# Other landing times in the planner's model, and value loads behind the loads of q and k

## The chip, the cores and the metric

The kernel runs on one core of a Trainium2 chip. The core has five engines with an instruction stream each: PE (TensorE, matrix products), DVE (VectorE), ACT (ScalarE), POOL (GpSimd) and SP (SyncE, which here issues nearly all DMAs). Each takes its instructions in the order in which the program gives them, and waits at semaphores for the others. The metric is the device time of one execution in microseconds (us), the median of several runs.

## The reference

Thresholded attention, and after it a SwiGLU network on its output. q, k and v have 8 batches, 8 heads, 576 rows and 64 columns in float32; the network has 4608 tokens, a width of 512 and an inner width of 1536.

```python
scores = scale * np.matmul(q, k.transpose(0, 1, 3, 2))
thresh = np.max(scores, axis=-1, keepdims=True) - tau
scores = np.where(scores >= thresh, scores, -1000000000.0)
scores = scores - np.max(scores, axis=-1, keepdims=True)
attn = np.exp(scores)
attn = attn / (np.sum(attn, axis=-1, keepdims=True) + 1e-09)
x = np.matmul(attn, v)          # then heads side by side: (B * S, H * D)

xn = x / np.sqrt(np.mean(x * x, axis=-1, keepdims=True) + 1e-06) * rms_g
g, val = xn @ w_gate, xn @ w_val
out = (g * (1.0 / (1.0 + np.exp(-g))) * val) @ w_out
```

## The kernel before

**Steps.** The rows of attention are cut into 36 chunks of 128: four of each batch, and for each pair of batches one "virtual" chunk that holds the last 64 rows of both. A chunk times a pair of heads is a step, so there are 144 steps, numbered from 0. A step's score product runs on PE into PSUM (`emit_burst`, L680; `s_ps`). From step 32 on the scores of all steps are laid end to end and cut into bursts of 1024 columns. DVE scales a burst into `ssb` and keeps the row extreme (L713). POOL makes the threshold (`nth`, L754), ACT applies it and the exponential (L765, L769, L772), or for a third of the steps ACT makes the exponential (L784) and POOL the mask (L798, L803). The weights, `wsb` in float16, are turned by a DMA transposition on SP (L832; in the first 16 steps on PE, L817) into `wt`. Every second step PE multiplies two steps' `wt` by the values `va` (`emit_av`, L850 and L855), and DVE divides by the row sums (L872, L874). When a chunk has all its heads, ACT squares it (L896), POOL makes and applies the norm (L899 to L904), and a DMA transposition (L908) puts it into `xnT`. Groups of 2 or 4 chunks then go through the network on PE: gate (L962), value (L967) and output products (L1033; for the last group L1008 too), with ACT's tanh (L976), DVE's products (L979, L984) and evictions (L1046, L1048), and a store on SP (L1054, L1058).

**Inputs of a batch.** `emit_batch_inputs(b)` is called two batches ahead, and its loads are gated on score steps from the first step of batch b - 1 on. From batch 2 on (`BLOCKED = 2`) k comes in four loads of 288 KB and q in four more, in an order that DVE can turn by 32x32 blocks (`emit_block_loads`, L369). The turns (`emit_blocks`: `turn_k` L382, `turn_kt` L387, `turn_q` L392) are made once for each of four pairs of heads, and each waits for all four loads of its tensor. The values come in four loads of 256 KB (`load_block`, L589) and small ones for the last 64 rows (`load_tail`, L604), and POOL casts them to float16 (L565). Each of the four casts of a batch waits for all four loads, which in their turn wait for the previous batch's casts. The network's weights come in twelve loads of 512 KB at the start (L1099) and are cast by POOL (L1106).

**The order.** Every operation is an `Op` with an engine, a cost, a priority and its dependencies. `order_ops` (L55) walks through a model of the chip: at each moment it takes for every engine the operation that can start soonest, the lowest priority number first where several can, and gives it a start and an end. The order so found is the order of the instructions on each engine; the model's times decide nothing else. `RANK` adds a number to the priorities by engine and kind of operation (from priority 8 on). A priority counts score steps for the most part, so a number of some hundreds puts a kind ahead of, or behind, nearly all others. `gated(o, step)` adds to an operation the dependency on the score burst of the step int(step): its loads can't start before that. A DMA's end in the model is the time when a single shared transfer queue has done it, and a constant on top: `LAT_TR` for transpositions, `LAT_LD` for those marked `bulk`, 2000 ns for others. Bulk loads are held while the shared queue is over `BACKLOG` behind.

```python
if o.dma:
    dma_free = max(dma_free, t + 300.0) + o.dma
    o.end = max(dma_free, t + o.cost) + (LAT_TR if o.cost == COST["sp_tr"] else LAT_LD if o.bulk else 2000.0)
```

So the model says when a DMA's data are there, and whatever is placed behind on an engine's stream waits on the chip if they come later.

Of the kernel before, what the change touches and what calls it, by code (L numbers as in the profile page):

```python
# [17 lines left out]
    evac_qk=600.0, evac_qk_act=465.0, evac_half=252.0, evac_kt=330.0, evac_kt_act=252.0, prelu=667.0, exp2=1060.0, exp1=666.0, exp0=590.0,  # L18
    mask_d=680.0, mask_g=1810.0, take_g=1360.0, trw=510.0, evac_w=400.0, evac_wp=900.0, rz=210.0, xmul=341.0, sq=612.0, xn=773.0,
    pool_tiny=302.0, pool_mean=944.0, pool_dma=880.0, cast_v=620.0, cast_vt=475.0, cast_w=665.0,  # L20
    sp=420.0, sp_v=600.0, sp_w=600.0, sp_tr=1300.0, sp_qk=680.0, sp_tl=630.0, sp_qb=600.0, turn=600.0, turn_t=200.0, turn_q=665.0,
)
DMA_NS = dict(qkb=1900.0, qk=1250.0, tl=700.0, v=880.0, vt=350.0, wt=1700.0, xt=800.0, out=800.0, w=820.0, wo=2500.0)
SWITCH = 125.0

RANK = dict(
    ACT={"emit_ffn/ev": 120, "emit_ffn/store": 100, "emit_ffn/tanh": -230, "emit_k_tail/ev": -80, "emit_q_tail/ev": 170, "emit_qk/ev": 60,
        "emit_softmax/ex": -50, "emit_softmax/ex2": -210, "emit_softmax/prelu": -20, "emit_x/sq": -200},
    DVE={"emit_av/half": -4.4, "emit_blocks/turn_k": 2, "emit_blocks/turn_kt": 3, "emit_blocks/turn_q": 3, "emit_burst/ttr": -7.5, "emit_ffn/ev": 60,
        "emit_ffn/gate": -1.3, "emit_ffn/silu": -6.8, "emit_k_tail/ev": -90, "emit_qk/ev": -150, "emit_softmax/ev": 270},  # L30
    PE={"emit_av/fn": -190, "emit_burst/fn": -160, "emit_ffn/gmm": 5, "emit_ffn/omm": 12, "emit_ffn/vmm": -10, "emit_k_tail/tr": 10, "emit_q_tail/tr":
        -50, "emit_qk/tr": 80, "emit_softmax/tr": -220},
    POOL={"emit_softmax/mask": 50, "emit_softmax/nthr": -320, "emit_softmax/take": -150, "emit_x/mean": -50, "emit_x/norm": -80, "round_/<lambda>":
        -57, "main/<lambda>": 520, "main/cast": -360},
)


class Op:
    __slots__ = ("eng", "cost", "prio", "deps", "fn", "ring", "frees", "slot", "end", "start", "dma", "opens", "nring", "mode", "bulk", "release", "pick", "quad")

    def __init__(self, eng, cost, prio, deps, fn, ring=None, frees=None, dma=0.0, nring=1, mode=0, bulk=False):
        self.eng, self.cost, self.prio, self.fn = eng, cost, prio, fn
        self.deps = [d for d in deps if d is not None]
        self.ring, self.frees, self.dma = ring, frees, dma
        self.slot = self.end = self.start = None
        self.opens = ()
        self.nring = nring
        self.mode = mode
        self.bulk = bulk
        self.release = 0.0  # L50
        self.pick = None
        self.quad = False


def order_ops(ops, ring_sizes):  # L55


    import heapq

    for o in ops:  # L60
        if o.prio >= 8.0 and o.eng != "SP":
            path = o.fn.__qualname__.split(".")
            o.prio += RANK.get(o.eng, {}).get((path[-3] if path[-3].startswith(("emit", "load", "setup", "transposed", "round")) else "main") + "/" + path[-1], 0.0)

    ring_free = {r: [(0.0, i) for i in range(n)] for r, n in ring_sizes.items()}
    users = {}
    left = {}
    for i, o in enumerate(ops):
        left[i] = len(o.deps)
        for d in o.deps:  # L70
            users.setdefault(id(d), []).append(i)
    pending = {}
    for i, o in enumerate(ops):
        pending.setdefault(o.eng, [])
        if not left[i]:
            pending[o.eng].append(i)
    eng_free = {e: 700.0 for e in pending}
    dma_free = 0.0
    mode = 0
    out = []  # L80
    ready_at = {i: 0.0 for i in range(len(ops))}
    while len(out) < len(ops):
        best = None
        for e, lst in pending.items():
            if not lst:
                continue
            t0 = eng_free[e]
            cand = None
            opts = []
            for i in lst:  # L90
                o = ops[i]
                t = max(t0, ready_at[i])
                if o.ring is not None:
                    free = [f for f in ring_free[o.ring] if f[1] in (o.pick or SLOTS)]
                    if len(free) < o.nring:
                        continue
                    t = max(t, sorted(free)[o.nring - 1][0])
                other = e == "PE" and o.mode != mode
                t = max(t, o.release)
                if o.bulk:  # L100
                    t = max(t, dma_free - BACKLOG)
                t += BIAS if other else 0.0
                opts.append((t, o.prio, i))
            if opts:
                soon = min(opts)[0] + HOLD.get(e, 0.0)
                cand = min((x for x in opts if x[0] <= soon), key=lambda x: (x[1], x[0], x[2]))
            if cand is not None and (best is None or cand < best[0]):
                best = (cand, e)
        (t, _, i), e = best
        o = ops[i]  # L110
        cost = o.cost
        if e == "PE":
            if o.mode != mode:
                t -= BIAS
                cost += SWITCH
            mode = o.mode
        o.start = t
        if o.ring is not None:
            o.slot = []
            for _ in range(o.nring):  # L120
                got = min(f for f in ring_free[o.ring] if f[1] in (o.pick or SLOTS))
                ring_free[o.ring].remove(got)
                o.slot.append(got[1])
            if o.pick:
                o.slot.sort()
        eng_free[e] = t + cost
        if o.dma:
            dma_free = max(dma_free, t + 300.0) + o.dma
            o.end = max(dma_free, t + o.cost) + (LAT_TR if o.cost == COST["sp_tr"] else LAT_LD if o.bulk else 2000.0)
        else:  # L130
            o.end = t + cost
        if o.frees is not None:
            ring_free["R"].append((o.end + LAT[o.eng], o.frees[0].slot[o.frees[1]]))
        for slot in o.opens:
            ring_free["R"].append((o.end + LAT[o.eng], slot))
        pending[e].remove(i)
        out.append(o)
        for j in users.get(id(o), []):
            u = ops[j]
            wait = 60.0 if o.dma else SELF[o.eng] if u.eng == o.eng else LAT[o.eng]  # L140
            ready_at[j] = max(ready_at[j], o.end + wait)
            left[j] -= 1
            if not left[j]:
                pending[u.eng].append(j)
    return out
# [3 lines left out]
def kernel(  # L149
# [17 lines left out]
    NP = H // 2  # L167
# [80 lines left out]
    def gated(o, step):  # L248
        gates.append((o, step))
        return o  # L250
# [16 lines left out]
    for s, (ci, p) in enumerate(steps):  # L267
        kind, b, _ = chunks[ci]
# [90 lines left out]
    def emit_block_loads(b, prio):  # L359

        los = {}
        for j, src in ((1, k), (0, q)):
            before = turned[j] if turned else [x for t in tr_of for x in t[-NQK:]] + ([] if j else tail_load["use", 0])
            for h in range(2):
                for e in range(2):
                    def load(o, j=j, src=src, h=h, e=e):
                        rows = slice(64 * h + 32 * e, 64 * h + 32 * e + 32)
                        heads = src[b, NP * h:NP * h + NP, :, 32 * e:32 * e + 32]
                        nc.sync.dma_start(out=kx[rows] if j else qx[rows], in_=heads.rearrange("a (s r) d -> s r a d", r=RUN)  # L369
                                          if j else heads.rearrange("a (r s) d -> s a r d", r=RUN))  # L370

                    pr = prio + BLOCK_STEP * len([x for y in los.values() for x in y])
                    los.setdefault(j, []).append(gated(add("SP", COST["sp_qb"], pr, before, load, dma=DMA_NS["qkb"], bulk=True), pr))
        turned[:] = [[], []]
        return los

# [180 lines left out]
    def emit_v(b, prio):  # L557
# [10 lines left out]
        def free(p):  # L568
            return [o_v] + last_av.get((b - 2, p), [])

        for p in range(NP):
# [12 lines left out]
            if b >= BLOCKED and p == 0:  # L584
                lo = []
                for g in range(4):
# [2 lines left out]
                        nc.sync.dma_start(out=vst8[32 * g:32 * g + 32].rearrange("s h (c d) -> s h c d", d=D),  # L589
                                          in_=v[b].rearrange("h (s r) d -> s h r d", r=RUN)[:, :, at:at + 4])  # L590

                    lo.append(gated(add("SP", COST["sp_v"], pr + V_STEP * g, v_cast[-NP:], load_block, dma=DMA_NS['v'], bulk=True), pr + V_STEP * g))
            ca = add("POOL", COST["cast_v"], (pr + 1 if b else p - 1.0), lo + free(p), round_(
                t[:, p, 0:8, 0:D].rearrange("q (c h) d -> q h c d", h=2),
                nat.rearrange("q h (c d) -> q h c d", d=D)))
            v_cast.append(ca)
# [495 lines left out]
    for c in range(DFF // 512):  # L1092
        for d in range(0, 4, 2):
            for w_dram, w_sb in ((moe_w_gate, wg), (moe_w_val, wv)):
# [5 lines left out]
                        "(e p) n -> p e n", p=128))  # L1100

                lo = gated(add("SP", COST["sp_w"], pr, w_use[slot], load, dma=2 * DMA_NS['w'], bulk=True), pr)
                w_use[slot] = []
                for e in range(2):
                    def cast(o, d=d, w_sb=w_sb, c=c, slot=slot, e=e):
# [71 lines left out]
PART_PRIO = 2.0  # L1177
SIZES = (2, 2, 4, 4, 4, 4, 4, 4, 4, 4)
LAG = 8.0
LAT_TR = 3000.0  # L1180
LAT_LD = 2000.0
REL = (0.0, 0.0)
REL_N = (0, 0)
# [17 lines left out]
NSTAGE = 3  # L1201
NQK = 3
BLOCKED = 2
BLOCK_STEP = 1.5
V_STEP = 1.5
W_FROM = 2.0
W_STEP = 0.4
N_XPE = 0
# [41 lines left out]
```

## Time and profile before

| | us |
|---|---|
| median of 13 runs | 562.21 |
| lowest and highest of them | 558.0 and 565.13 |
| the profiled execution | 558.0 |
| its span | 556.1 |

The span is the time from the first to the last instruction of the program in the trace. PE is busy for 528.5 us of it, DVE 463.9, ACT 424.3, POOL 256.0. A transfer's time "to landing" runs from its issue on SP to the last byte. "Idle before" is the time for which an engine stood still just ahead of an instruction, put down to what came last. Matmul ends are modelled, so PE's holes are read from the starts of the matmuls.

### The profile page before, as it was taken

The page shows a single profiled execution, that of the slowest core. Times are in us where ns is not written, and L with a number is a line of the kernel's source. Part 1 is how long each engine was busy: PE and PEld are TensorE (multiplying, and loading weights), DVE is VectorE, ACT ScalarE, POOL GpSimd, SP SyncE. Part 2 cuts the span into 40 slices and gives each one's busy share as a digit, 9 for nine tenths or more (in the row PEclk, how much of TensorE's full clock was granted, in tenths as well). Part 3 has the DMA queues.
Part 4 walks back from the last instruction along what each step waited for, and adds up shares of the span by engine and source line. Part 5 has one row for each costly group of instructions (what it writes and reads, how often), then busy time and mean ns, then how long its engine had stood idle before and what let it go on. Part 6 is the DMA issues. An engine that isn't in the chain of part 4 may idle for free.

```text
span 556.1 us, 14272 instructions
## 1 busy us (share of the span) xinstructions
PE 528.5 (95%) x5336; PEld 277.9 (50%) x5336; DVE 463.9 (83%) x1342; ACT 424.3 (76%) x648; POOL 256.0 (46%) x418
## 2 busy tenths in 40 slices
PE   8989999896998999899999999999999999999997
PEld 4765656553554554454444444544454545445443
DVE  4997989674999798888998899879987997995481
ACT  5998988577897787958895798877976897994230
POOL 2377823473446544355446455364435535361100
PEclk9999999998999999999999999999999999999999
DMA  9999999989999998999999799999999667575202
GB/s 212 241 296 275 161 143 173 171 158 155 164 171 145 158 159 151 183 176 176 172 177 181 161 150 156 179 214 152 148 187 191 139 101 135 98 112 118 86 1 77
DMA packets 325318, 89.03 MB, mean 160 GB/s; under 512 B 307840, under 2 KB 317568, under 8 KB 325248
## 3 DMA queue, kind: packets, MB, share of 16 engines
q1 hardware_dynamic: 322320, 85.76, 91.2%
q0 software_dynamic: 1600, 1.57, 1.9%
q8 instruction: 42, 0.69, 0.6%
q10 hardware_dynamic: 1328, 0.79, 0.5%
q14 instruction: 28, 0.23, 0.1%
HBM read 37.75 MB, written 9.44 MB: 85 GB/s over the span
## 4 chain that ended last, share of the span: by engine, by line
PE 48%; DVE 15%; DMA 10%; ACT 5%; issue 3%; SPq 2%; POOL 2%; DVEq 0%; POOLq 0%; ACTq 0%
PE s_ps L680 14%; PE ring L1033 9%; PE ring L967 8%; PE ring L962 8%; DVE ssb L713 8%; DMA wt<-wsb 4%; DMA qkx<-in_q_dram 4%; PE ring L855 3%; PE s_ps L1008 2%; ACT ssb L765 2%; DVE sl L979 2%; DVE qkt L392 1%; PE s_ps L1033 1%; PE ring L850 1%; ACT wsb L772 1%
## 5 line engine op out<-in xcount | busy, mean ns | idle before, releaser
L765 ACT ACTIVATE ssb<-ssb,nth 128x576 f32<-128x576 f32 x246 | 180.2, 766 | 28.5 <-POOL nth L754 28.4
L680 PE MATMUL s_ps<-qkt 64*64 64x288 f32 (+9 forms) x2240 | 177.2, 415 | 11.2 <-DVE mxp L713 7.2
L713 DVE CUSTOM_DVE_ANT_0 ssb<-s_ps,zrow 128x576 f32<-128x576 f32 (+8 forms) x288 | 170.6, 635 | 11.3 <-PE s_ps L680 6.1
L772 ACT ACTIVATE wsb<-ssb 128x1152 f16<-128x1152 f32 x102 | 118.0, 1157 | 16.1 <-DMA wt<-wsb 15.1
L680 PEld LDWEIGHTS s_ps<-qkt 64*64 64x64 f32 (+1 forms) x2240 | 84.7, 135 | 77.6 <-issue 26.7
L967 PE MATMUL ring<-xnT,wv 128*128 128x512 f16 (+1 forms) x460 | 108.1, 357 | 1.7 <-DVE sl L979 1.0
L754 POOL TENSOR_SCALAR nth<-mx 128x2 f32<-128x2 f32 x144 | 31.6, 219 | 168.4 <-DVE mx L713 163.4
L962 PE MATMUL ring<-xnT,wg 128*128 128x512 f16 (+1 forms) x460 | 108.0, 357 | 0.9 <-DVE sl L979 0.7
L798 POOL TENSOR_SCALAR wsb<-ssb,nth 128x576 f16<-128x576 f32 x42 | 72.5, 1726 | 23.0 <-DMA wt<-wsb 18.0
L976 ACT ACTIVATE th<-ring 128x512 f32<-128x512 f32 (+1 forms) x115 | 61.8, 539 | 24.6 <-PE ring L962 24.5
L979 DVE SCALAR_TENSOR_TENSOR sl<-th,ring 128x512 f32<-128x512 f32 (+1 forms) x115 | 71.1, 621 | 8.0 <-ACT th L976 8.0
L713 DVE CUSTOM_DVE_ANT_0 ssb<-s_ps,zrow,mxp 128x128 f32<-128x128 f32 (+7 forms) x112 | 52.9, 510 | 21.1 <-PE s_ps L680 21.0
L962 PEld LDWEIGHTS <-wg 128*128 128x128 f16 x480 | 44.2, 98 | 52.1 <-issue 10.4
L967 PEld LDWEIGHTS <-wv 128*128 128x128 f16 x480 | 43.7, 98 | 53.1 <-issue 14.6
L803 POOL TENSOR_TENSOR wsb<-wsb,esb 128x576 f16<-128x576 f16 x42 | 53.8, 1280 | 3.4
L855 PE MATMUL ring<-va,wt 128*128 128x65 f16 (+1 forms) x1280 | 51.5, 193 | 0.0
L855 PEld LDWEIGHTS <-wt 128*128 128x128 f16 (+1 forms) x1280 | 46.3, 100 | 7.7 <-issue 3.8
L1033 PE MATMUL ring<-wo,hf 128*128 128x512 f16 x204 | 47.2, 379 | 2.1 <-DVE xsb L874 1.7
L784 ACT ACTIVATE esb<-ssb,nth 128x576 f16<-128x576 f32 x42 | 32.3, 770 | 15.9 <-POOL nth L754 15.8
L850 PE MATMUL ring<-va,wt 128*128 128x130 f16 (+1 forms) x160 | 32.2, 224 | 6.8 <-DVE sl L979 3.4
L984 DVE TENSOR_TENSOR hf<-ring,sl 128x512 f16<-128x512 f32 (+1 forms) x59 | 36.6, 627 | 1.9
L984 DVE TENSOR_TENSOR stg<-ring,sl 128x512 f16<-128x512 f32 (+1 forms) x56 | 34.4, 625 | 2.3 <-PE ring L967 0.5
(73 smaller groups left out, 499.3 us busy)
## 6 DMA issues: line engine op xcount, KB each, us to landing
vst<-in_v_dram SPq DMA_DIRECT2D x32, 256.0 KB, 4.5
out_dram<-osb SPq DMA_DIRECT2D x29, 256.0 KB, 2.5
qkx<-in_k_dram SPq DMA_DIRECT2D x24, 288.0 KB, 4.7
qkx<-in_q_dram SPq DMA_DIRECT2D x24, 288.0 KB, 5.2
stg<-in_moe_w_gate_dram SPq DMA_DIRECT2D x6, 512.0 KB, 6.3
stg<-in_moe_w_val_dram SPq DMA_DIRECT2D x6, 512.0 KB, 6.2
wt<-wsb SPq DMA_TRANSPOSE x128, 4.0
qkx<-in_k_dram SPq DMA_DIRECT2D x7, 256.0 KB, 4.9
```

The costliest lines, as they stand in the source:

```text
L680: nc.tensor.matmul(s_ps[h][rows, at:at + hi - lo], lhs(hs), k_of(bb, p, h)[hs, lo:hi], start=True, stop=True)
L713: nc.vector.tensor_tensor_reduce(out=ssb_of(s)[:, h, lo:hi], in0=s_ps[h][:, at:at + hi - lo], in1=zrow[:, lo:hi], scale=-1.0 / 8.0, scalar ...
L765: nc.scalar.activation(out=sb_[:, h], in_=sb_[:, h], func=PRELU, scale=-1.0, bias=nth[m][:, h:h + 1], **PRELU_KW)
L772: nc.scalar.activation(out=wsb[s % NW], in_=sb_, func=AF.Exp)
L798: nc.gpsimd.tensor_scalar(out=wsb[s % NW][:, h], in0=sb_[:, h], scalar1=nth[m][:, h:h + 1], scalar2=None, op0=ALU.is_le)
L855: nc.tensor.matmul(ring[o.slot[0]][rs, at:at + D + 1], w[:, 5 * h + j, rs], va[vi][:, p, 2 * j + h], start=False, stop=(h == 1 and j == 3))
L962: nc.tensor.matmul(ring[o.slot[0]][:, 0:n], wg[d][:, fs], xnT[slot][:, d, 0:n], start=(d == 0), stop=(d == 3))
L967: nc.tensor.matmul(ring[o.slot[0]][:, 0:n], wv[d][:, fs], xnT[slot][:, d, 0:n], start=(d == 0), stop=(d == 3))
L976: nc.scalar.activation(out=th[i][:, 0:n], in_=ring[g.slot[0]][:, 0:n], func=AF.Tanh, scale=0.5)
L979: nc.vector.scalar_tensor_tensor(out=sl[i][:, 0:n], in0=th[i][:, 0:n], scalar=1.0, in1=ring[g.slot[0]][:, 0:n], op0=ALU.add, op1=ALU.mult)
L984: nc.vector.tensor_tensor(out=hf[hi][:, 0:n], in0=ring[vv.slot[0]][:, 0:n], in1=sl[i][:, 0:n], op=ALU.mult)
L1033: nc.tensor.matmul(ring[(first or o).slot[0]], hf[hs[fc][0]][:, 128 * j:128 * (j + 1)], wo[:, fc], start=(fc == 0), stop=(fc == NFC - 1))
```

## The change

The planner's model gets a landing time for each kind of load: `Op` has a field `lat`, with new constants for the block loads of q and k (`LAT_QB`, 4500 ns), of values (`LAT_V`, 4000) and of the network's weights (`LAT_W`, 3000), all 2000 before. `LAT_TR` goes from 3000 to 2000. The value loads of a batch are gated `V_FROM` = 6 steps later and then one step apart instead of 1.5; the block loads of q and k stand 1.4 steps apart instead of 1.5. The casts of the values get a priority `V_CAST` = 9 later instead of 1, from batch 2 on. Two costs of the model change slightly, and all numbers of `RANK`. No instruction computes anything else than before.

```diff
-    ... turn_t=200.0, turn_q=665.0,
+    ... turn_t=210.0, turn_q=680.0,
 RANK = dict(
-    ACT={"emit_ffn/ev": 120, "emit_ffn/store": 100, "emit_ffn/tanh": -230, "emit_k_tail/ev": -80, "emit_q_tail/ev": 170, "emit_qk/ev": 60,
-        "emit_softmax/ex": -50, "emit_softmax/ex2": -210, "emit_softmax/prelu": -20, "emit_x/sq": -200},
-    DVE={"emit_av/half": -4.4, "emit_blocks/turn_k": 2, "emit_blocks/turn_kt": 3, "emit_blocks/turn_q": 3, "emit_burst/ttr": -7.5, "emit_ffn/ev": 60,
-        "emit_ffn/gate": -1.3, "emit_ffn/silu": -6.8, "emit_k_tail/ev": -90, "emit_qk/ev": -150, "emit_softmax/ev": 270},
-    PE={"emit_av/fn": -190, "emit_burst/fn": -160, "emit_ffn/gmm": 5, "emit_ffn/omm": 12, "emit_ffn/vmm": -10, "emit_k_tail/tr": 10, "emit_q_tail/tr":
-        -50, "emit_qk/tr": 80, "emit_softmax/tr": -220},
-    POOL={"emit_softmax/mask": 50, "emit_softmax/nthr": -320, "emit_softmax/take": -150, "emit_x/mean": -50, "emit_x/norm": -80, "round_/<lambda>":
-        -57, "main/<lambda>": 520, "main/cast": -360},
+    ACT={"emit_ffn/ev": 260, "emit_ffn/store": 60, "emit_ffn/tanh": -350, "emit_k_tail/ev": -140, "emit_q_tail/ev": -100, "emit_qk/ev": 280,
+        "emit_softmax/ex": 18, "emit_softmax/ex2": -350, "emit_softmax/prelu": 18, "emit_x/sq": -320},
+    DVE={"emit_av/half": -10.4, "emit_blocks/turn_k": 30, "emit_blocks/turn_kt": 20, "emit_blocks/turn_q": 50, "emit_burst/ttr": -14.1, "emit_ffn/ev":
+        140, "emit_ffn/gate": -80, "emit_ffn/silu": -13.4, "emit_k_tail/ev": -130, "emit_qk/ev": -100, "emit_softmax/ev": 410},
+    PE={"emit_av/fn": -260, "emit_burst/fn": -160, "emit_ffn/gmm": 18.5, "emit_ffn/omm": 22, "emit_k_tail/tr": 250, "emit_q_tail/tr": -200,
+        "emit_qk/tr": 170, "emit_softmax/tr": -190},
+    POOL={"emit_softmax/mask": 110, "emit_softmax/nthr": -180, "emit_softmax/take": -170, "emit_x/mean": -60, "emit_x/norm": -41, "round_/<lambda>":
+        -47.8, "main/<lambda>": 670, "main/cast": -260},
 )
...
+        self.lat = LAT_TR if cost == COST["sp_tr"] else LAT_LD if bulk else 2000.0
...
-            o.end = max(dma_free, t + o.cost) + (LAT_TR if o.cost == COST["sp_tr"] else LAT_LD if o.bulk else 2000.0)
+            o.end = max(dma_free, t + o.cost) + o.lat
...
                     los.setdefault(j, []).append(gated(add("SP", COST["sp_qb"], pr, before, load, dma=DMA_NS["qkb"], bulk=True), pr))
+                    los[j][-1].lat = LAT_QB
...
-                    lo.append(gated(add("SP", COST["sp_v"], pr + V_STEP * g, v_cast[-NP:], load_block, dma=DMA_NS['v'], bulk=True), pr + V_STEP * g))
-            ca = add("POOL", COST["cast_v"], (pr + 1 if b else p - 1.0), lo + free(p), round_(
+                    pl = pr + V_FROM + V_STEP * g
+                    lo.append(gated(add("SP", COST["sp_v"], pl, v_cast[-NP:], load_block, dma=DMA_NS['v'], bulk=True), pl))
+                    lo[-1].lat = LAT_V
+            ca = add("POOL", COST["cast_v"], (pr + V_CAST if b >= BLOCKED else pr + 1 if b else p - 1.0), lo + free(p), round_(
...
+                lo.lat = LAT_W
...
-LAT_TR = 3000.0
+LAT_TR = 2000.0
...
-BLOCK_STEP = 1.5
-V_STEP = 1.5
+BLOCK_STEP = 1.4
+V_STEP = 1.0
+V_FROM = 6.0
+V_CAST = 9.0
+LAT_QB = 4500.0
+LAT_V = 4000.0
+LAT_W = 3000.0
```

More of the change, by code (lines that the diff above doesn't have):

```diff
@@ L20 @@
     pool_tiny=302.0, pool_mean=944.0, pool_dma=880.0, cast_v=620.0, cast_vt=475.0, cast_w=665.0,
-    sp=420.0, sp_v=600.0, sp_w=600.0, sp_tr=1300.0, sp_qk=680.0, sp_tl=630.0, sp_qb=600.0, turn=600.0, turn_t=200.0, turn_q=665.0,
+    sp=420.0, sp_v=600.0, sp_w=600.0, sp_tr=1300.0, sp_qk=680.0, sp_tl=630.0, sp_qb=600.0, turn=600.0, turn_t=210.0, turn_q=680.0,
 )
@@ L26 @@
 RANK = dict(
-    ACT={"emit_ffn/ev": 120, "emit_ffn/store": 100, "emit_ffn/tanh": -230, "emit_k_tail/ev": -80, "emit_q_tail/ev": 170, "emit_qk/ev": 60,
-        "emit_softmax/ex": -50, "emit_softmax/ex2": -210, "emit_softmax/prelu": -20, "emit_x/sq": -200},
-    DVE={"emit_av/half": -4.4, "emit_blocks/turn_k": 2, "emit_blocks/turn_kt": 3, "emit_blocks/turn_q": 3, "emit_burst/ttr": -7.5, "emit_ffn/ev": 60,
-        "emit_ffn/gate": -1.3, "emit_ffn/silu": -6.8, "emit_k_tail/ev": -90, "emit_qk/ev": -150, "emit_softmax/ev": 270},
-    PE={"emit_av/fn": -190, "emit_burst/fn": -160, "emit_ffn/gmm": 5, "emit_ffn/omm": 12, "emit_ffn/vmm": -10, "emit_k_tail/tr": 10, "emit_q_tail/tr":
-        -50, "emit_qk/tr": 80, "emit_softmax/tr": -220},
-    POOL={"emit_softmax/mask": 50, "emit_softmax/nthr": -320, "emit_softmax/take": -150, "emit_x/mean": -50, "emit_x/norm": -80, "round_/<lambda>":
-        -57, "main/<lambda>": 520, "main/cast": -360},
+    ACT={"emit_ffn/ev": 260, "emit_ffn/store": 60, "emit_ffn/tanh": -350, "emit_k_tail/ev": -140, "emit_q_tail/ev": -100, "emit_qk/ev": 280,
[6 more added lines that the diff above has]
+        -47.8, "main/<lambda>": 670, "main/cast": -260},
 )
 class Op:
-    __slots__ = ("eng", "cost", "prio", "deps", "fn", "ring", "frees", "slot", "end", "start", "dma", "opens", "nring", "mode", "bulk", "release", "pick", "quad")
+    __slots__ = ("eng", "cost", "prio", "deps", "fn", "ring", "frees", "slot", "end", "start", "dma", "opens", "nring", "mode", "bulk", "release", "pick", "quad", "lat")
     def __init__(self, eng, cost, prio, deps, fn, ring=None, frees=None, dma=0.0, nring=1, mode=0, bulk=False):
```

## The prediction

> **What bounds the kernel now.** I read the page first (engines, slices, DMA issues), then the waits by engine, then the timeline wherever PE stood still.
>
> ```profile
> span 556.1 us, 14272 instructions
> ...
> PE 528.5 (95%) x5336; PEld 277.9 (50%) x5336; DVE 463.9 (83%) x1342; ACT 424.3 (76%) x648; POOL 256.0 (46%) x418
> ...
> DMA  9999999989999998999999799999999667575202
> ...
> vst<-in_v_dram SPq DMA_DIRECT2D x32, 256.0 KB, 4.5
> ...
> qkx<-in_q_dram SPq DMA_DIRECT2D x24, 288.0 KB, 5.2
> ...
> wt<-wsb SPq DMA_TRANSPOSE x128, 4.0
> ```
>
> PE is nearly full, and the DMA engines are as full until the last loads. So no engine has spare work to lose: a gain has to come out of PE's holes. Adding up every place where a matmul starts over 0.25 us later than the columns of the one before it account for gives 26.8 us, of which 21.5 us lie between 84 and 440 us, where the loads run. Three kinds stand out.
>
> First, loads that land on the dot. On DVE, on POOL, and SP's queue before them (timeline rows: start, length, instruction, idle before it):
>
> ```profile
> 105.86 0.78 DVE L392 STREAM_TRANSPOSE qkt<-qkx 128x576 f32<-128x576 f32 x1 [3.73 <-DMA qkx<-in_q_dram]
> ```
> ```profile
> 301.07 2.76 DVE L392 STREAM_TRANSPOSE qkt<-qkx 128x576 f32<-128x576 f32 x4 [2.59 <-issue]
> ```
> ```profile
> 298.99 1.80 POOL L565 TENSOR_SCALAR va<-vst 128x512 f16<-128x512 f32 x3 [1.91 <-DMA vst<-in_v_dram]
> ```
> ```profile
> 294.92 0.58 SPq L589 DMA_DIRECT2D vst<-in_v_dram  x1
> 295.55 0.46 SPq L369 DMA_DIRECT2D qkx<-in_q_dram  x1
> 296.18 4.84 SPq L832 DMA_TRANSPOSE wt<-wsb  x2
> ```
>
> Batch 5's last value load and last q load are issued side by side at 294.9 and 295.6 us. They land at 298.75 and 300.99; the cast starts at 298.99 and the turn of q at 301.07. So it is in nearly every batch: the last q lands at 105.83, 173.15, 245.12, 300.99, 372.38, 427.45 us and the first turn starts at 105.86, 173.34, 245.20, 301.07, 372.84, 427.53. The "issue" that ends the 2.59 us is that landing. DVE's idle time before these turns is 3.73, 0.35, 1.94, 2.59, 0 and 0.07 us.
>
> Second, a place with no filler (stretches: length; busy us by engine; granted clock; DMA):
>
> ```profile
> 126.00:129.50 3.50, 0.91 (x10) 0.46 (x6) 2.56 (x11) 1.97 (x3) 1.64 (x4) 1.00 0.92 190
> 129.50:132.30 2.80, 2.78 (x50) 2.19 (x50) 0.75 (x3) 2.77 (x5) 2.63 (x2) 1.00 1.07 181
> 132.30:135.00 2.70, 0.16 (x6) 0.03 (x2) 2.67 (x13) 2.13 (x4) 0.82 (x3) 1.00 0.81 136
> 135.00:139.00 4.00, 3.94 (x18) 1.41 (x19) 0.36 (x4) 2.14 (x3) 0.00 (x0) 0.57 1.16 153
> ```
> ```profile
> 129.52 2.23 PE L680 MATMUL s_ps<-qkt 64*64 64x384 f32 x32 [2.62 <-DVE mxp L713]
> ...
> 135.06 3.68 PE L680 MATMUL s_ps<-qkt 64*64 64x512 f32 x16 [2.60 <-DVE mxp L713]
> ```
>
> Around steps 39 and 40 score bursts follow each other with nothing, or only attention times values, between. PE waits twice for DVE to empty the scores' PSUM, and then the granted clock falls to 0.57 for 4 us; a burst that takes 1.89 us elsewhere takes 3.68.
>
> Third, PE waiting for a transposed weight tile, still small:
>
> ```profile
> L850 PE MATMUL ring<-va,wt x160: 217/220/245, 19.3 to 513.2; 128*128 128x130 f16 x128, 128*64 128x130 f16 x32
> ...
>   DMA wt<-wsb: 5.2, 9
> ```
>
> **What the Trainium skill says.** [...]"DMA: Bandwidth & Descriptors", Queues, rings and completion order: SP has one ring on each DMA engine, consumed in order, so a transposition of SP stands behind SP's loads; here they take 3.2 us at the least, 4.0 in the median, 8.7 at most. "TensorE: Matmul & The Clock Gate", What's actually happening: the array's clock is halved after an idle window of about 3.4 us; the 0.57 after holes of 2.6 us twice agrees.
>
> **The change part by part.** No instruction's arithmetic changes; only the order and the gates do. Compared step by step, 439 of 593 PE steps, 711 of 864 on DVE and 194 of 321 on SP move, on PE mostly by up to three places.
>
> *q earlier (counted 6.7 us from issue at the least instead of 4.2; measured 5.2).* The value loads leave the gaps between the q loads. Counting by score step, the last q load of batches 2 to 7 stood behind transposition 24, 43, 64, 80, 101, 116 and now behind 24, 41, 61, 77, 97, 113. The first turn of q stood behind eviction 29, 49, 69, 85, 106, 120 and now behind 29, 47, 67, 83, 103, 119. The distance was 5, 6, 5, 5, 5, 4 steps and is 5, 6, 6, 6, 6, 6. A step is 3.6 us (some 520 us over 144), so one step more covers the waits of batches 4 and 5 (1.94, 2.59). What PE lost to them is 1.5 us at 250 us and 0.43 + 0.48 us at 306 to 307.5: -2.4 us. Batch 2 keeps its distance, but its last q has no value load straight before it; I count part of its holes (1.6 and 0.7 at 105 to 108) with those after the turns of batches 3, 6 and 7 (1.8, 1.2, 1.2, 0.8): -1.5 us out of 7, bounds 0 and -5.
>
> *The place without filler.* Before step 40's burst there now stand a gate and a value product, 8 matmuls of 216 ns, 1.7 us that came later. Step 39 stays bare. The hole shrinks by 1.7 us unless their xnT is late (it landed at 133.4, so 1 us of it would stay). If the clock then stays up, 1.8 us more. I take -3.0; bounds -1.7 and -4.6.
>
> *Early filling.* Between steps 15 and 33 one more FFN product (4 x 109 ns) and six more output products (6 x 216 ns) are done, less a transposition that moves away: -1.2 us if they fall into the early holes, 0 if DVE, which evicts them, was the limit there.
>
> *Attention times values sooner.* The transpositions' constant falls from 3.0 to 2.0 us; the planner thus counts 4.0 us from issue at the least and no longer 5.0. The measured median is 4.0, so half of them are now later than counted. In the new order these matmuls stand on average 1.4 us of PE work nearer to their burst, since bursts move back. I took for the 64 groups from step 17 on the start of the first matmul on the pair's second tile less that tile's landing: a tenth have under 0.26 us, a quarter under 1.2, half under 2.2. Pulling all of them 0.5 us forward costs the sum of the shortfalls, 3.3 us; 1.0 us costs 9.4. Cover that hides it: none, PE is full. I take 0.5, because transpositions land after 3.6 to 3.9 us where no loads run against 4.2 to 4.8 where they do, and loads no longer pair up: +3.3, bounds 0 and +9.4.
>
> *Values later (counted at least 5.2 us instead of 3.2; measured 4.5).* From last load to first cast there were 6, 4, 4, 4, 3, 4 steps and are 4, 3, 3, 4, 6, 4 (batch 3's other casts 5). POOL already idled 0.5 to 1.9 us at these casts. Queued behind them are the thresholds (L754), and ACT's prelu waits for those. A threshold late by 3.25 us at 221 us (tail values) left PE holes of 1.2, 0.5 and 0.7 us. Attention times values itself has many steps to spare. +1.0 us; bounds 0 and +3.
>
> *The rest.* PE changes mode 162 times instead of 157, about 0.1 us each (the median gap into a burst): +0.5. Weight loads keep their order and stay hidden behind the first bursts; uncovered they would cost at most POOL's 4.3 us of waits for them.
>
> Sum: -2.4 -1.5 -3.0 -1.2 +3.3 +1.0 +0.5 = -3.3 us. The profiled execution took 558.0 us (span 556.1), the lowest of 13; the median is 562.2. The difference carries over: **558.9 us**.
>
> **Rivals.**
> *Transpositions become the bound (slower).* Place: the wait of L850 for wt. All 64 groups lose the full 1.0 us that the constant gives away: +9.4, with +3 at the casts, +0.5, and -8.1 of gains: +4.8, 567 us. For it: a median landing equal to the count leaves no margin, and the order really moves. Against: loads bunch less. With the other terms as taken it decides from a pull of about 0.8 us on.
> *Nothing comes of it (same).* The q turns are no longer late, but DVE then waits for PE instead (it already does for 27 us before L713), and the casts take the place of the turns: 562 us.
> *More than I count.* All batch holes go with the q waits (-7 rather than -3.9), the clock stays up (-4.6), the transpositions land as counted (+1): about -11, 551 us. Against: holes at 222 and 370 us come from tail values and from output stores, which the change doesn't aim at.
>
> **How the numbers follow.** Forecast, a gain of 2 to 8 us: 0.41. More: 0.15. Same, within 0.3% or 1.7 us, about what a measurement of this kernel can tell from no change: 0.17. Slower: 0.27. So faster 0.56, same 0.17, slower 0.27. The range runs from 549.5 (a little past the larger gain) to 568 (past the slower case), leaving out about 1 in 10 at each end; the forecast's own range is 554 to 560.5.
>
> **What would show it.** Right: no DVE idle time over 1 us before L392 in batches 4 to 7; one hole, not two, near steps 39 and 40, and no stretch at clock 0.57; more waits of L850 for wt than 5.2 us, but under 9. Wrong: L850's waits over 12 us; POOL idle over 10 us before L565, with ACT's waits for the thresholds grown from 44 us; or new bare bursts, which the order does not show.

## The result, and the profile after

The changed kernel takes 557.03 us (median of 11 runs, 553.69 to 560.02) against 562.27 for the kernel before (48 runs). The ratio is 0.9898, with a 95% interval from 0.9877 to 0.9919: 5.2 to 5.7 us faster, depending on whether medians or the ratio are taken. A second comparison, further down, gave 0.9873 (0.9837 to 0.9910). The profiled execution took 556.28 us, its span 554.5. Since the profiled execution before was the fastest of its runs, the two profiles lie only 1.7 us apart, and they are compared here mainly by kinds of waits. A second profile of the changed kernel (after_again, 553.4 us) is used where one profile misleads.

The page of the changed kernel:

```profile
span 554.5 us, 14260 instructions
...
PE 523.2 (94%) x5336; PEld 274.9 (50%) x5336; DVE 467.7 (84%) x1342; ACT 427.0 (77%) x648; POOL 255.9 (46%) x418
...
DMA  8999999989999999999999699999999676754102
...
vst<-in_v_dram SPq DMA_DIRECT2D x32, 256.0 KB, 4.6
...
qkx<-in_q_dram SPq DMA_DIRECT2D x24, 288.0 KB, 5.4
...
wt<-wsb SPq DMA_TRANSPOSE x128, 3.9
```

Amounts of work and transfers are the same, and the landing times hardly differ: 4.6 for 4.5, 5.4 for 5.2, 3.9 for 4.0 us. The loads did not become quicker by being spread; they are asked for at other moments. (Lines shift: L392 is now L394, L565 L567, L713 L717, L850 and L855 are L854 and L859, L872 L876, L962 L966.)

The turns of q of batch 5 and its first casts, on DVE's and POOL's timelines (start, length, instruction, idle before it):

```profile
288.09 2.09 DVE L394 STREAM_TRANSPOSE qkt<-qkx 128x576 f32<-128x576 f32 x3
```
```profile
301.44 1.80 POOL L567 TENSOR_SCALAR va<-vst 128x512 f16<-128x512 f32 x3 [0.52 <-DMA out_dram<-osb]
```

No turn of any batch has idle time before it any more; the last q of batch 5 lands at 286.05, 2 us before its turn (in batches 2 to 7 0.4 to 5.1 us before). The idle time that stood there, 8.6 us over the six batches, is gone. The casts, later as they are, wait less than before: POOL's idle time before L567 is 9.0 us against 14.8.

What has come in its place is seen in the query for PE's value matmuls:

```profile
L854 PE MATMUL ring<-va,wt x158: 217/221/290, 18.8 to 507.6; 128*128 128x130 f16 x126, 128*64 128x130 f16 x32
...
  DMA wt<-wsb: 31.2, 27
```

This counts weight loads and matmuls together, 16.5 and 14.7 us, and stood at 5.2; in the second profile it is 19.6. The worst place, on PE's timeline and in stretches (length; busy us by engine; granted clock; DMA):

```profile
216.39 0.41 PE L859 MATMUL ring<-va,wt 128*128 128x65 f16 x8
219.60 0.29 PE L854 MATMUL ring<-va,wt 128*128 128x130 f16 x1 [2.81 <-DMA wt<-wsb]
219.69 0.64 PE L859 MATMUL ring<-va,wt 128*128 128x65 f16 x8
220.26 3.04 PE L684 MATMUL s_ps<-qkt 64*64 64x512 f32 x24
```
```profile
216.60:219.30 2.70, 0.20 (x7) 0.07 (x3) 1.65 (x5) 2.70 (x5) 0.81 (x3) 0.96 1.42 180
219.30:222.70 3.40, 3.10 (x29) 1.58 (x33) 1.77 (x4) 3.40 (x6) 0.17 (x1) 0.53 1.27 176
```

Between the two tiles of one group PE stands still for 2.8 us until the second tile has landed, and after that the clock is halved for a stretch. Summing holes over 0.25 us as in the prediction gives 28.7 us for this profile, no less than the 26.8 before; a second profile of the changed kernel gives 22.5. So one profile's sum of holes is too rough to carry a verdict of 1%, and the experiments below are judged by their ratios.

### The profile page after: what moved, and what is told of

It is laid out like the page before. It is cut to its first block, busy times and chain, and to the rows that moved or that the text cites. A ratio compares the mean times of both kernels' runs of the same rounds, so it can differ in the third digit from the quotient of the medians.

```text
span 554.5 us, 14260 instructions
## 1 busy us (share of the span) xinstructions
PE 523.2 (94%) x5336; PEld 274.9 (50%) x5336; DVE 467.7 (84%) x1342; ACT 427.0 (77%) x648; POOL 255.9 (46%) x418
## 4 chain that ended last, share of the span: by engine, by line
PE 49%; DMA 17%; ACT 10%; DVE 9%; issue 6%; POOL 6%; SPq 2%; POOLq 0%; DVEq 0%; ACTq 0%
PE s_ps L684 14%; DMA wt<-wsb 12%; PE ring L966 9%; PE ring L1037 9%; PE ring L971 9%; DVE ssb L717 4%; ACT ssb L769 4%; ACT wsb L776 3%; PE ring L859 3%; PE s_ps L1012 2%; DMA qkx<-in_q_dram 2%; ACT th L980 1%; DVE sl L983 1%; POOL va L567 1%; DMA xnT<-xn 1%
## 5 line engine op out<-in xcount | busy, mean ns | idle before, releaser
L717 DVE CUSTOM_DVE_ANT_0 ssb<-s_ps,zrow 128x576 f32<-128x576 f32 (+8 forms) x288 | 171.4, 635 | 10.9 <-PE s_ps L684 7.5
L684 PE MATMUL s_ps<-qkt 64*64 64x288 f32 (+9 forms) x2240 | 172.0, 417 | 3.5 <-DVE mxp L717 2.6
L684 PEld LDWEIGHTS s_ps<-qkt 64*64 64x64 f32 (+1 forms) x2240 | 81.9, 136 | 68.4 <-issue 29.5
L966 PE MATMUL ring<-xnT,wg 128*128 128x512 f16 (+1 forms) x464 | 109.1, 357 | 3.2 <-DMA xnT<-xn 3.2
L983 DVE SCALAR_TENSOR_TENSOR sl<-th,ring 128x512 f32<-128x512 f32 (+1 forms) x116 | 72.5, 627 | 14.2 <-ACT th L980 13.7
L717 DVE CUSTOM_DVE_ANT_0 ssb<-s_ps,zrow,mxp 128x128 f32<-128x128 f32 (+7 forms) x112 | 53.3, 512 | 20.2 <-PE s_ps L684 19.7
L966 PEld LDWEIGHTS <-wg 128*128 128x128 f16 x480 | 43.7, 98 | 52.0 <-issue 10.5
L859 PE MATMUL ring<-va,wt 128*128 128x65 f16 (+1 forms) x1264 | 52.0, 194 | 0.0
L1037 PE MATMUL ring<-wo,hf 128*128 128x512 f16 x216 | 49.8, 379 | 0.0
L859 PEld LDWEIGHTS <-wt 128*128 128x128 f16 (+1 forms) x1280 | 46.9, 100 | 4.6
L854 PE MATMUL ring<-va,wt 128*128 128x130 f16 (+1 forms) x158 | 31.9, 225 | 14.7 <-DMA wt<-wsb 14.7
L988 DVE TENSOR_TENSOR stg<-ring,sl 128x512 f16<-128x512 f32 (+1 forms) x57 | 35.7, 627 | 2.8 <-PE ring L971 0.2
```

The source lines that it names most:

```text
L684: nc.tensor.matmul(s_ps[h][rows, at:at + hi - lo], lhs(hs), k_of(bb, p, h)[hs, lo:hi], start=True, stop=True)
L717: nc.vector.tensor_tensor_reduce(out=ssb_of(s)[:, h, lo:hi], in0=s_ps[h][:, at:at + hi - lo], in1=zrow[:, lo:hi], scale=-1.0 / 8.0, scalar ...
L859: nc.tensor.matmul(ring[o.slot[0]][rs, at:at + D + 1], w[:, 5 * h + j, rs], va[vi][:, p, 2 * j + h], start=False, stop=(h == 1 and j == 3))
L966: nc.tensor.matmul(ring[o.slot[0]][:, 0:n], wg[d][:, fs], xnT[slot][:, d, 0:n], start=(d == 0), stop=(d == 3))
L983: nc.vector.scalar_tensor_tensor(out=sl[i][:, 0:n], in0=th[i][:, 0:n], scalar=1.0, in1=ring[g.slot[0]][:, 0:n], op0=ALU.add, op1=ALU.mult)
L988: nc.vector.tensor_tensor(out=hf[hi][:, 0:n], in0=ring[vv.slot[0]][:, 0:n], in1=sl[i][:, 0:n], op=ALU.mult)
```

## The experiments

All ratios are to the kernel before, timed on the same chip in the same session. Two kinds of edit occur. In one a constant is changed and the order is planned anew, so that many other steps move too. In the other the finished order is taken and single operations are moved in one engine's list, with all dependencies and turns at PSUM slots kept; nothing else moves. The second kind comes closer to isolating a cause. In their diffs the helper `moved` is given in words, as a comment. The mean granted clock of the runs is named where it bears on a reading (0.994 for the kernel before in all three sessions of the experiments); what it is worth stands in the last section.

**Value loads behind q, alone.** On the kernel before:

```diff
     seq = order_ops(ops, {"R": 4})
+    # batches 2 to 7: the four value loads go behind the last q load on SP,
+    # one other issue between each; their four casts eight places later on POOL
+    seq = moved(seq)
```

> The order of the kernel before, with the value loads of batches 2 to 7 moved behind the last q load of their batch on SP (one transposition or other issue between each) and their casts eight places later on POOL; PE, DVE and ACT keep their order. Theory that the q turns waited because of the value loads beside them: DVE's idle time before L392 falls from 8.7 us to under 3, time 558 to 560. Rival (q is late because SP reaches it late, behind transpositions that wait for their data): idle time stays over 6 us, time 561 to 564. If the casts become late: over 564, with POOL idle over 10 us before L565.

Measured: 0.9921 (0.9890 to 0.9951), 555.84 us against 559.92. DVE's idle time before the turns is 0. SP and DVE of this kernel around batch 5 (L440 is the q load, L660 the value load, L463 the turn):

```profile
291.86 0.57 SPq L440 DMA_DIRECT2D qkx<-in_q_dram  x1
292.48 1.79 SPq L660 DMA_DIRECT2D vst<-in_v_dram  x1
294.44 1.29 SPq L903 DMA_TRANSPOSE wt<-wsb  x1
```
```profile
297.17 2.75 DVE L463 STREAM_TRANSPOSE qkt<-qkx 128x576 f32<-128x576 f32 x4
```

The last q load stands behind the same transposition in SP's list as before. It now comes 1.4 us after that one's issue instead of 2.0, since no value load stands between, and lands after 4.6 us instead of 5.4: together 6.0 for 7.5 us in this batch, 6.6 for 10.1 in batch 2, 5.6 for 8.4 in batch 3. (The times themselves also differ because this kernel is some microseconds ahead by here.) Twenty-four loads and twenty-four casts moved, PE's, DVE's and ACT's lists are untouched, and most of the change's gain is there: 0.8% (0.5 to 1.1) of its 1.0%. The theory held and its rival fell. The gain, about 4.4 us, is over the 2 to 4 us that were expected, and it isn't the clock's: that is 0.993. The shares of loads and casts were not told apart by a run. POOL's idle time before the casts fell as well, from 14.8 to 6.2 us, but what that could have freed, the thresholds, did not come sooner: ACT waits 51.8 us for them, against 44.2 before.

**The loads' part, planned anew.** The changed kernel with `RANK`, the turn costs and `LAT_TR` of before:

```diff
-    ... turn_t=210.0, turn_q=680.0,
+    ... turn_t=200.0, turn_q=665.0,
-RANK = ...            # the changed kernel's
+RANK = ...            # that of the kernel before
-LAT_TR = 2000.0
+LAT_TR = 3000.0
```

> The changed kernel with RANK, the two turn costs and LAT_TR as before: only the landing times and gates of loads are new; planned anew. Theory that the loads' order brings the gain: idle time before the turns 0 to 1 us, waits of attention times values for wt under 4 us, 0.985 to 0.992 of the kernel before, at least as fast as the changed kernel (0.990). Theory that the priorities bring it: 0.997 or more.

Measured: 0.9886 (0.9840 to 0.9932). The turns don't wait, and the kernel is not told apart from the changed one.

**The priorities, alone.** The kernel before with the new `RANK` and turn costs:

```diff
-RANK = ...            # that of the kernel before
+RANK = ...            # the changed kernel's
-    ... turn_t=200.0, turn_q=665.0,
+    ... turn_t=210.0, turn_q=680.0,
```

> The kernel before with the new RANK and turn costs alone; loads, landing times and LAT_TR as before; planned anew. Theory that the loads' order brings the gain: the turns still wait (6 us or more), 0.997 to 1.005. Theory that the priorities bring it: 0.993 or less.

Measured: 1.0071 (1.0052 to 1.0089), slower, and a little outside what either theory allowed. The turns of k and q wait 2.5 us (of q alone 1.4), less than the 6 expected, and yet time is lost. Two things have grown: ACT waits 67.1 us for the thresholds, against 44.2 before, and the mean clock over the 20 runs is 0.987 instead of 0.994, which by the slope in the last section goes with 2.6 of the 4 us. Which of them costs the time is not shown; b_v_behind has 51.8 us of the first and is fast. Together with loads_only this says that the priorities bring nothing by themselves; the loads do.

**The transpositions' constant, on the kernel before and undone on the changed one.**

```diff
-LAT_TR = 3000.0
+LAT_TR = 2000.0
```

> The kernel before with LAT_TR at 2000 alone, planned anew. Margin theory: waits for wt grow from 1.9 us to 10 or more and the time from 562 to 567 to 573. Exchange theory: 560 to 564. If LAT_TR brought the gain: 557 or less.

Measured: 1.0053 (1.0035 to 1.0071), some 3 us slower. The answer on the value matmuls has this line, 5.2 before:

```profile
  DMA wt<-wsb: 23.8, 24
```

The waits came as expected; the loss is at the low side, 3 us against 5 to 11. Undone on the changed kernel (the diff the other way round):

> The changed kernel with LAT_TR back at 3000, everything planned anew. Margin theory: waits for wt under 6 us, time 548 to 553, unless the new order has bare bursts. Exchange theory: 555 to 559. If LAT_TR was the part that brought the gain: 560 or more.

Measured: 0.9891 (0.9861 to 0.9921), not told apart from the changed kernel. PE's matmuls no longer wait for wt at all, but PE's waits before score bursts have come back: the line below, against 2.6 us in the changed kernel (3.8 in its second profile).

```profile
PE s_ps L684 <- DVE mxp L717: 12.1, 8, 2.6
```

So the constant costs when it is changed alone, and is neither gain nor loss in the whole. (The mean clock of the 4 runs is 0.989, against 0.992 of the changed kernel in the result; part of what the waits gave back may have gone there.)

**Attention times values later, by hand.** In the changed kernel's order 47 of the 72 groups go behind the network product that follows them on PE:

```diff
     seq = order_ops(ops, {"R": 4})
+    # PE's list: [.. emit_av, emit_ffn ..] becomes [.. emit_ffn, emit_av ..]
+    seq = moved(seq)
```

> The changed kernel's order, with 47 of the attention-times-values groups moved behind the one network product that follows them on PE; nothing else moves. Margin theory (the changed kernel's holes on PE are attention times values waiting for its second transposed tile, because the planner now counts 1 us less for it): the waits of these matmuls for wt fall from 14.7 us to about 5, and the time from 557 us to 547 to 551. Rival, exchange theory (PE's holes are set by DVE and ACT, and a hole closed here opens elsewhere): the waits fall, but the time stays at 555 to 558.

Measured: 0.9867 (0.9818 to 0.9917), waits for wt 7.8 us for 14.7. That looked like a gain over 0.9898, but the two numbers are from different sessions. So the changed kernel, the same edit, the edit with up to two products, and the edit on loads_only were timed together on one chip:

> The changed kernel itself, beside the next three on one chip: 0.988 to 0.992 of the kernel before, as in the result.

> The kernel of av_later once more, beside the changed one. Margin theory: 2 to 4 us under the changed kernel, as the holes before its transposed tiles are 7 us smaller and other holes took back part. Exchange theory: within 1 us of it.

> The changed kernel's order with attention times values behind up to two network products, so some 0.9 us more of margin for about 34 groups. Margin theory: waits for wt under 3 us, another 2 us off av_later. Exchange theory: the weights' buffers and the rows for the network come free later, so that time stays as in av_later or rises by 1 to 3 us.

> The kernel of loads_only (loads' order and landing times new, priorities and LAT_TR as before) with attention times values behind one network product (49 groups). Margin theory: its 7.8 us of waits for wt fall to about 3, 2 to 3 us off, 0.984 of the kernel before or less. Exchange theory: 0.987 to 0.990.

| | ratio | 95% interval | PE's matmuls waiting for wt, us | DVE's reciprocal waiting for PE, us |
|---|---|---|---|---|
| changed kernel | 0.9873 | 0.9837 to 0.9910 | 8.9 | 3.9 |
| one product later | 0.9887 | 0.9857 to 0.9917 | 7.7 | 9.4 |
| up to two later | 0.9896 | 0.9869 to 0.9923 | 3.9 | 17.0 |
| loads_only (an earlier session) | 0.9886 | 0.9840 to 0.9932 | 7.8 | 2.7 |
| loads_only, one product later | 0.9972 | 0.9952 to 0.9992 | 2.0 | 16.2 |

The last column is in the waits of the kernel with up to two products (L946 is the reciprocal that divides the group's result):

```profile
DVE rz L946 <- PE ring L929: 17.0, 22, 2.5
...
PE ring L924 <- DMA wt<-wsb: 3.9, 4, 2.0
```

and in those of the changed kernel in its second profile:

```profile
PE ring L854 <- DMA wt<-wsb: 8.9, 10, 3.0
...
DVE rz L876 <- PE ring L859: 3.9, 6, 1.6
```

The margin theory fell: with 5 us less waiting on PE the kernel is no faster, and on loads_only the edit loses nearly all of the gain. The clock doesn't explain it: up to two products later it is 0.994 against 0.991 for the changed kernel, which should make the former faster, and from loads_only to its edit it falls from 0.996 to 0.993, worth 1 us of 5. A likely way is visible: the group moved on PE, but its reciprocal kept its place on DVE, so DVE, which works in order, now waits where PE waited, and evictions and silu stand behind it. This was not tested by moving the reciprocal too, so whether the waits for wt could be taken away at a gain is open; tr_3000, where both are planned together, says that the gain then is not large. No version tried is shown to beat the changed kernel.

**The place without filler, alone, and with the value loads.** On the kernel before, one score burst moves on PE:

```diff
     seq = order_ops(ops, {"R": 4})
+    # PE's list: [.. burst of step 40, gate, value ..] becomes [.. gate, value, burst of step 40 ..]
+    seq = moved(seq)
```

> The order of the kernel before with one move on PE: the score burst that ends step 40 goes behind the gate and value product that follow it. Filler theory, as in the prediction: the second of the two holes near 126 to 135 us shrinks from 2.8 us by 1.7 us, and the 3.4 us at half clock that follow go away (1.7 us more): -1.7 to -3.4 us, 0.994 to 0.997 of the kernel before. Exchange theory (the hole opens elsewhere): within 0.2%, and the half-clock stretch may stay.

Measured: 0.9978 (0.9953 to 1.0002), about 1.2 us, and not certain. PE's timeline (L754 is the score burst):

```profile
129.87 3.91 PE L754 MATMUL s_ps<-qkt 64*64 64x384 f32 x32 [2.62 <-DVE mxp L787]
...
137.09 2.08 PE L754 MATMUL s_ps<-qkt 64*64 64x512 f32 x16 [0.89 <-DVE mxp L787]
```

The second hole has shrunk from 2.60 to 0.89 us as worked out. In this profile a half-clock stretch stands one burst sooner, after the first hole, and that burst took 3.91 us. But one profile doesn't settle it: over the 20 runs the mean clock is 0.997, against 0.994 over 44 runs of the kernel before. That is one such stretch less in a run, and by the slope in the last section about 1.1 us, as much as the whole gain. So it is open whether the shorter hole brought anything beside the clock. With the value loads moved too, and step 37's burst one product sooner:

> The order of the kernel before, value loads behind q and casts later as in b_v_behind, step 40's burst behind the gate and value product as in b_fill, and the burst that ends step 37 ahead of the output product before it, so that the burst of step 39 has that product before it. If the terms add: b_v_behind's 0.992, less 2 to 3.4 us of filler, less up to 1.3 us for the last move: 0.984 to 0.988 of the kernel before. If they don't: 0.990 to 0.993.

Measured: 0.9911 (0.9880 to 0.9942), not told apart from 0.9921 with the value loads alone (in another session). The terms do not visibly add.

## Why the prediction was right, and where its steps were not

The direction, the time (558.9 forecast, 557.03 measured) and the range held. The gain of 5.2 us is over the forecast 3.3. That the sum came near is partly luck: terms missed in both directions, and one of the signs that were to show it wrong came true (waits for wt over 12 us). By the terms of the sum:

*q earlier, -2.4 and -1.5.* Right in mechanism and near in size: removing the value loads from between the q loads gives -4.4 us alone (b_v_behind), casts included. The prediction said "one step more covers the waits". For the changed kernel this fits: in batches 4 to 7 its last q takes 5.6 to 6.9 us from issue to landing, longer than the 4.9 to 5.4 before, and is in time because it stands further ahead of its turn. But the step more is not needed: b_v_behind kept the old distance and the waits went as well. There it was time within a place of the list, SP's issue of the value load ahead and a shorter landing. Without that load the last q landed 1.0 to 3.5 us sooner after its transposition in batches 2 to 6.

*Place without filler, -3.0.* The hole went as worked out (-1.7), and the measured -1.2 us (+0.1 to -2.6) falls short of -3.0. How it splits into hole and clock is open, since the clock's part alone could be the whole of it. In the changed kernel the two holes measure 2.6 and 1.0 us. The sign "no stretch at clock 0.57" holds in its first profile and fails in its second, where the burst after the same first hole runs at half clock:

```profile
124.35 2.23 PE L684 MATMUL s_ps<-qkt 64*64 64x384 f32 x32 [2.62 <-DVE mxp L717]
```
```profile
125.80 3.92 PE L684 MATMUL s_ps<-qkt 64*64 64x384 f32 x32 [2.62 <-DVE mxp L717]
```

Both profiles have further stretches, after the waits for wt near 217 and 401 us. Set beside the kernel before in one session, the changed kernel's mean clock is lower, 0.991 against 0.994; so by the slope in the last section the clock as a whole took some 1 us instead of giving 1.8.

*Attention times values sooner, +3.3.* Two steps failed. One is "I take 0.5". The margin from the landing of a pair's second tile to the matmul that reads it fell from a median of 2.17 us to 1.2 in one profile of the changed kernel and 1.55 in the other, so by 1.0 and 0.6 us, and landing times did not shorten. The waits of the matmuls rose from 2.3 us to 14.7 and 8.9: by 12.4 us, more than the upper bound of 9.4, and by 6.6, twice the 3.3 that was taken. Counted with the weight loads, as in the prediction's sign "under 9", they are 31.2 and 19.6 us. Transpositions straight behind a load in SP's queue are the slow ones: in the first profile they land after 5.0 us in the median, all others after 3.6, and 8 of its 13 waits were for such ones, which had taken 4.9 to 6.5. The other step is "Cover that hides it: none, PE is full". The rise did not go into the time one for one: in b_tr_2000 these waits grew by 8.7 us and the time by 3, and on the changed kernel undoing the constant takes them away and brings nothing. The +3.3 met the 3 us of that run by two errors against each other. The rival "transpositions become the bound" asked for the whole length of the waits in time and fell.

*Values later, +1.0.* At the casts wrong in sign. Steps between last load and first cast were counted from two lists and came out smaller, but POOL's waits before the casts fell from 14.8 to 9.0 us; in the profile the first cast starts 0.1 to 5.0 us after the last landing, against at most 0.4 us before in batches 3 to 7. ACT's waits for the thresholds, through which the term was to cost time, did grow, from 44.2 to 49.3 us. What both are worth in time was not measured.

*Early filling, -1.2, and the mode changes, +0.5.* Neither was measured by itself. The scores of the first 39 steps, with the same network work done by then, end 5.2 us sooner in the changed kernel's first profile (125.9 against 131.1 us) and 2.5 us sooner in its second, where half-clock stretches begin at 78 and 126 us. Of the holes that were named, only the 2.3 us at batch 2's turn lie before that point; the second hole near step 40 and the stretch behind it come later. So the filling may have had a part, and its size is open.

## What to carry to other kernels

When an engine that works in order waits for a load that lands on the dot, look at what its issuing queue does just before: a load for a later consumer that stands between the parts of an urgent one can make that one late (here by 1.0 to 3.5 us), and moving it behind is a change of one queue, and of the place of its consumer. A hole on a full engine need not be worth its length; before pricing a new wait at its length, ask which engine would wait there otherwise, and whether the consumers have to move along with the producer. Terms read off one profile don't add up when the order is planned anew, and two profiles of one kernel can differ in the very thing that is to be read from them: compare a quantity over all runs where there is one, as with the clock.

## What was not expected of the hardware

The half-clock stretches are 3.41 us long each (two run together as 6.83 in some profiles), and most come after holes of 2.0 to 3.0 us. How many occur varies from run to run of one kernel and goes with its time: over 44 runs of the kernel before in one session the time falls by 0.36 us for each 0.001 of mean granted clock (correlation -0.55), over 22 in another by 0.40 (-0.75), over 27 in the third by 0.33 (-0.42). One stretch takes 0.003 off the mean clock, so it goes with 1.0 to 1.2 us. This is a correlation, and the holes before the stretches are in it. In the six runs of the changed kernel in the last comparison the difference is larger than that price: 555.2 and 557.3 us at a clock of 0.987, 551.2 to 551.9 at 0.991 to 0.994.

The Trainium skill ("TensorE: Matmul & The Clock Gate", What's actually happening) puts the window at 3413 ns and calls it free-running. The traces agree: in each of the 14 profiles the stretches start whole multiples of 3.413 us apart (54.0 between the two of the changed kernel's first profile, 14.0, 27.0 and 54.0 in its second). They lie on a grid that the work does not shift, and a hole counts by how it falls on the grid. The hole of 2.62 us ahead of step 39's burst is the example. In the kernel before it is divided between two windows of the grid, and the clock stays up; in the changed kernel's second profile it lies in one, and the next window runs at half clock (length; busy us of PE first):

```profile
124.82:128.23 3.41, 2.08 (x17) 1.46 (x16) 1.99 (x6) 1.88 (x5) 1.71 (x5) 1.00 0.70 156
128.23:131.64 3.41, 2.12 (x32) 1.57 (x32) 1.51 (x8) 3.41 (x5) 2.19 (x3) 1.00 0.91 143
```
```profile
122.72:126.13 3.41, 0.79 (x10) 0.41 (x7) 2.81 (x12) 3.18 (x5) 1.74 (x5) 1.00 0.85 187
```

Over the 14 profiles 30 stretches begin after the first 12 us and while PE has work left. In 28 of the windows before them PE is busy for less than 44% (in the other two for 51 and 69%); of the 2134 other windows at full clock in that time none is below 44%. So no idle window of 3.4 us is needed, and the prediction's "agrees" was too much: the page speaks of a whole idle window, and here holes of 2 to 3 us were enough where they fell into one. How many half-clock stretches a kernel has is then in part chance, run by run.
